# Loading one block of wo into lanes 0 to 63 by eleven small transfers

## The chip, the cores and the metric

The kernel runs on one core of one Trainium2 chip. The metric is the device time of one execution in microseconds (us). A core has five engines with an instruction queue each: TensorE (PE, with its weight loads as PEld), VectorE (DVE), ScalarE (ACT), GpSimd (POOL) and SyncE (SP). Data come from the chip's memory (HBM) into the on-chip SBUF, which has 128 lanes (partitions), by 16 DMA engines that work beside the five. SP and ACT start these transfers; each transfer is cut into packets, one for each contiguous piece.

## What is computed

One step of decoding for four sequences: attention over a cache of 4,096 keys and values with 32 heads of 128, beside a gated MLP, both added to the input.

```
xn  = layernorm(x)                                  # x: 4 x 640
q   = (xn @ wq) as 32 heads of 128
s   = q . k_cache * 128**-0.5                       # 4 x 32 x 4096
o   = softmax(s) . v_cache                          # 4 x 32 x 128
att = o.reshape(4, 4096) @ wo                       # wo: 4096 x 640
z   = gelu(xn @ w_in); z1, z2 = halves of z; z2 = layernorm(z2)
mlp = (z1 * (w_sp * z2 + b_sp)) @ w_out
out = x + att + mlp                                 # all inputs bfloat16
```

The two caches are 128 MiB each; all else together is some 14 MB. Every byte of them is read once.

## The kernel before

The heads are taken in eight groups of four (HG = 8, HT = 4). A tile is one group of one sequence: 32 tiles (NT) of K and 32 of V, each 128 lanes of 32,768 bytes (4,096 KB). They go through five buffers (KV_SLOTS) that K and V share. `load` issues one tile on SP's queue; `pump` issues the next ones of a fixed list as long as the buffer that each needs has been released (`used`).

The main loop runs over the 32 tiles i and is written out by hand for PE, DVE, ACT and SP. In each step DVE multiplies the K tile by the query and folds it in two halves (L400, L409), PE sums over the head dimension by matmuls with the identity (L418), DVE reduces (L429 to L442), ACT takes the exponentials (L453), and PE multiplies with an earlier V tile (`weighted`, L470). At the end of a step `pump` issues what has become possible.

Behind every fourth tile one group is finished. `group_pick` (L502) gathers its rows, `group_turn` (L513, L521) divides by the sum and transposes 32 by 32 on DVE, which leaves o_t with the head dimension on lanes, and `group_proj` (L530) multiplies by the group's 512 rows of wo and adds to out_ps, where x, the MLP and all groups are summed. The rows of one block of wo are spread so that lane p holds rows 4p to 4p+3: one contiguous piece of 5,120 bytes in each of 128 lanes (L155). `load_wo(j)` issues block j in step 4j+2, after `pump`; it has a pool of two buffers (WO_BUFS). The last block comes in four transfers, one for each head (L153), because the last group goes another way: the last V tile is loaded in four pieces (V_CUTS), its matmuls (L625) wait for each, and L530 follows.

Transfers that SP and ACT start use eight completion semaphores in turn; a transfer on a semaphore that is still in use by the one eight before it waits for that one to land.

Of the kernel before, what the change touches and what calls it, by code (L numbers as in the profile page):

```python
# [9 lines left out]
FP32 = mybir.dt.float32  # L10
BF16 = mybir.dt.bfloat16
# [3 lines left out]

KV_SLOTS = 5
EXTRA_K = (24, 28)
WO_BUFS = 2


@with_exitstack
def kernel(
# [14 lines left out]
    nc = tc.nc  # L37
    P = nc.NUM_PARTITIONS
    Bsz, Sq, D = A_x.shape
    _, H, S, Dh = A_k_cache.shape  # L40
# [8 lines left out]
    HT = 4  # L49
# [11 lines left out]
    NOH = D // 2  # L61
    QD = 32
# [5 lines left out]
    const = ctx.enter_context(tc.tile_pool(name="const", bufs=1))  # L68
    kv = ctx.enter_context(tc.tile_pool(name="kv", bufs=KV_SLOTS))
    wop = ctx.enter_context(tc.tile_pool(name="wop", bufs=WO_BUFS))  # L70
    work = ctx.enter_context(tc.tile_pool(name="work", bufs=1))
    small = ctx.enter_context(tc.tile_pool(name="small", bufs=2))
# [6 lines left out]
    def slot(name):  # L79
        return kv.tile([P, SLOT], BF16, tag="kv", name=name)  # L80

    x_bf = const.tile([Bsz, D], BF16)
    nc.scalar.dma_start(out=x_bf[:], in_=A_x.flatten_outer_dims())

    wq_v = A_wq.rearrange("(p c) n -> p c n", c=DC)
# [1 line left out]
    for c0, c1 in ((0, HT), (HT, DC)):  # L87
        t = slot("wq")[:, 0 : (c1 - c0) * HD].rearrange("p (c n) -> p c n", n=HD)
# [13 lines left out]
        out=w_out_sb[:, 0:NFF, :], in_=B_w_out[0 : NFF * P].rearrange("(p k) n -> p k n", k=NFF)  # L102
# [40 lines left out]
            n_loaded[0] += 1  # L143

    wo_tiles = {}

    def load_wo(j):
        wo_tiles[j] = wop.tile([P, HT, D], BF16, name="wo")
        rows = A_wo[j * HT * P : (j + 1) * HT * P]
        if j == HG - 1:  # L150
            by_head = rows.rearrange("(h p) n -> p h n", p=P)
            for hh in range(HT):
                nc.sync.dma_start(out=wo_tiles[j][:, hh, :], in_=by_head[:, hh, :])  # L153
            return
        nc.sync.dma_start(out=wo_tiles[j][:], in_=rows.rearrange("(p j) n -> p j n", j=HT))  # L155
# [2 lines left out]

    ident = const.tile([P, P], BF16)
    make_identity(nc, ident[:])  # L160
    ones_row = const.tile([1, P], FP32)
    nc.vector.memset(ones_row[:], 1.0)
    eps_tile = const.tile([P, 1], FP32)
    nc.vector.memset(eps_tile[:], eps)
    ones_sq = const.tile([P, P], FP32)
# [14 lines left out]
    for i in range(NSTAT):  # L180
# [5 lines left out]
        out=rstd[:], in_=mv[:, 1:2], func=ACT.Sqrt, bias=eps_tile[:Bsz], scale=1.0  # L186
# [4 lines left out]
        out=xn_bf[:],  # L191
# [9 lines left out]
    for c in range(DC):  # L201
        nc.tensor.transpose(
            out=xnT_ps[:, c, :], in_=xn_v[:, c, :], identity=ident[:Bsz, :Bsz]
# [7 lines left out]
    for r in range(QB):  # L211
        q_ps = ps_pv.tile([P, GW], FP32, tag="pv", name="q_ps")
        for c in range(DC):
            t, i = wq_parts[c]
            for g in range(CB):
                hg = r * CB + g
                nc.tensor.matmul(  # L217
                    out=q_ps[g * QD : (g + 1) * QD, :],
                    lhsT=xnT[:, c, :],
                    rhs=t[:, i, hg * GW : (hg + 1) * GW],  # L220
                    start=(c == 0),
                    stop=(c == DC - 1),
# [9 lines left out]
        out=hot[:],  # L232
        in_=ident[:].rearrange("p (g t m) -> p t m g", g=P // QD, t=2),
# [3 lines left out]
    for a in range(2):  # L237
        for t in range(2):
            nc.vector.tensor_copy(
                out=pick[:, a, :, :, 2 * a + t],  # L240
                in_=hot[:, t, :].rearrange("p (c h) -> p c h", c=CB),
# [8 lines left out]
    for half in range(2):  # L250
        nc.tensor.matmul(
            out=out_sum(half),
            lhsT=ident[:Bsz, :Bsz],
            rhs=x_bf[:, half * NOH : (half + 1) * NOH],
            start=True,
            stop=False,
# [11 lines left out]
    def gmlp():  # L268
        zz, gw, gt, gz, sq = (gm[n] for n in ("zz", "gw", "gt", "gz", "sq"))
        zT = ps_pv.tile([P, 2, NFC, Bsz], FP32, tag="pv", name="zT")  # L270
        for t in range(2):
            f1 = t * Fh + NFF * P
            w_t = w_in_sb[:, :, t * Fh : f1].rearrange("p c (f k) -> p c k f", k=NFF)
            for k in range(NFC):
                for c in range(DC):
                    nc.tensor.matmul(
                        out=zT[: P if k < NFF else FT, t, k, :],
                        lhsT=w_t[:, c, k, :] if k < NFF else w_in_sb[:, c, f1 : f1 + FT],
                        rhs=xnT[:, c, 0:Bsz],
                        start=(c == 0),  # L280
                        stop=(c == DC - 1),
# [5 lines left out]
            out=gw[:], in0=gw[:], scalar1=0.044715, scalar2=1.0, op0=ALU.mult, op1=ALU.add  # L287
# [3 lines left out]
            out=gt[:], in_=gw[:], func=ACT.Tanh, scale=math.sqrt(2.0 / math.pi)  # L291
        )
        nc.vector.tensor_scalar(
            out=gt[:], in0=gt[:], scalar1=1.0, scalar2=0.5, op0=ALU.add, op1=ALU.mult
# [5 lines left out]
        for src, at in ((gz[:, 1, :, :], 0), (sq[:], Bsz)):  # L300
            for k in range(NFC):
                nc.tensor.matmul(
                    out=s_ps[:, at : at + Bsz],
                    lhsT=ones_sq[:, 0:1],
                    rhs=src[:, k, :],
                    start=(k == 0),
                    stop=(k == NFC - 1),
                )
        st, ac = gm["st"], gm["ac"]
# [33 lines left out]
        )  # L343
        ac_ps = ps_m.tile([P, 2 * Bsz], FP32, tag="m", name="ac_ps")
        nc.tensor.matmul(
            out=ac_ps[:], lhsT=ones_row[:], rhs=ac[:], start=True, stop=True
        )
        ac_sb = work.tile([P, 2 * Bsz], FP32, name="ac_sb")
        nc.scalar.copy(out=ac_sb[:], in_=ac_ps[:])
# [161 lines left out]
    def group_turn(hg):  # L511
        o_n = small.tile([P, HT, QD], BF16, name="o_n")
        nc.vector.tensor_scalar(  # L513
            out=o_n[:].rearrange("p j q -> p q j"),
            in0=taken.pop(hg)[:].rearrange("p (q j) -> p q j", j=HT),
            scalar1=gr.pop(hg)[:, 0:1],
            scalar2=None,
            op0=ALU.mult,
        )
        o_t = small.tile([P, HT, QD], BF16, name="o_t")  # L520
        nc.vector.transpose(  # L521
            out=o_t[:].rearrange("p j q -> p (j q)"), in_=o_n[:].rearrange("p j q -> p (j q)")
        )
        gr[hg] = o_t[:, :, 0:Bsz]

    def group_proj(hg):
        o_n = gr.pop(hg)
        for hh in range(HT):
            for half in range(2):
                nc.tensor.matmul(  # L530
                    out=out_sum(half),
                    lhsT=o_n[:, hh, :],
                    rhs=wo_tiles[hg][:, hh, half * NOH : (half + 1) * NOH],
                    start=False,
                    stop=(hg == HG - 1 and hh == HT - 1),
                )
# [25 lines left out]
    with tc.manual_schedule(engines={E.PE, E.DVE, E.Activation, E.SP}):  # L562
        stage_q(0)
        stage_q(1)
        gmlp()
        used.update(occupants[:3])
        pump()
        for i in range(NT):
            j = turns.get(i)
            last = turns.get(i - 1, -1)  # L570
            product(i, 0)
            at(i - 1, row_sums, 1)
            at(i - 1, head_max)
            group(last, group_pick)
            fold_half(i, 0)
            at(i - 1, exps)
            sums(i, 0)
            group(last, group_turn)
            if i + 2 < NT:
                stage_q(i + 2)  # L580
            product(i, 1)
            due = [] if j is None else [j]
            if i == NT - 1:
                due += range(j + 1, NT - 2)
            for jj in due:
                consume(jj)
            row_sums(i, 0)
            fold_half(i, 1)
            sums(i, 1)
            group(last, group_proj)  # L590
            used.add(("k", i))
            pump()
            if i % Bsz == 2 and i // Bsz < HG - 1:
                load_wo(i // Bsz)
        load_wo(HG - 1)
        row_sums(NT - 1, 1)
        head_max(NT - 1)
        exps(NT - 1)
        hg, b = HG - 1, Bsz - 1
        o_ps = ps_m.tile([P, HT, Bsz], FP32, tag="m", name="o_last")  # L600

        def pick_last(a):
            o = taken.pop((hg, a))
            for c in range(CB):
                nc.tensor.matmul(
                    out=o_ps[:],
                    lhsT=o[:, c, :],
                    rhs=pick[:, a, c, :, 0:Bsz],
                    start=(a == 0 and c == 0),
                    stop=False,  # L610
                )

        pick_last(0)
        weighted(NT - 2, closing=True)
        take(hg, 1)
        den = ps_m.tile([P, HT, Bsz], FP32, tag="m", name="den_all")
        nc.tensor.matmul(
            out=den[:], lhsT=ones_sq[:], rhs=acc[hg % NACC][:, :, 0:Bsz], start=True, stop=True
        )
        rden = small.tile([P, HT, Bsz], FP32, name="rden_all")  # L620
        nc.vector.reciprocal(out=rden[:], in_=den[:])
        pick_last(1)
        pm = p_m[b][:].rearrange("p g (t c h) -> p g t c h", t=2, c=CB)
        for c in range(NC):
            nc.tensor.matmul(  # L625
                out=o_ps[:, :, b],
                lhsT=v_tiles[NT - 1][:, c, :],
                rhs=pm[:, c // CB, b % 2, c % CB, :],
                start=False,
                stop=(c == NC - 1),  # L630
            )
        o_n = small.tile([P, HT, Bsz], BF16, name="o_n_last")
        nc.vector.tensor_tensor(out=o_n[:], in0=o_ps[:], in1=rden[:], op=ALU.mult)
        gr[hg] = o_n
        group_proj(hg)

        res = work.tile([P, NOH], BF16, name="res")
        out_v = out.flatten_outer_dims()
        r0, r1 = slice(0, Bsz), slice(OG, OG + Bsz)
        nc.scalar.copy(out=res[r0], in_=out_ps[r0])  # L640
        nc.vector.tensor_copy(out=res[r1], in_=out_ps[r1])
        nc.scalar.dma_start(out=out_v[:, 0:NOH], in_=res[r0])
        nc.sync.dma_start(out=out_v[:, NOH:D], in_=res[r1])
# [30 lines left out]
```

## Time and profile before

| What | Value |
|---|---|
| Median of 3 runs (lowest, highest) | 666.81 us (666.65, 666.91) |
| The profiled execution, its own time | 666.78 us |
| Span of the profile, first to last instruction | 665.0 us |
| Busy: DVE, PE, ACT, POOL | 499.5, 309.9, 127.1, 4.7 us |
| HBM read over the span | 282.24 MB, 424 GB/s |
| K tiles: 32 transfers of 4,096 KB, issue to landing | 41.2 us (median) |
| V tiles: 31 transfers of 4,096 KB, issue to landing | 35.7 us (median) |
| wo blocks 0 to 6: 640 KB each, issue to landing | 42.3 us (median) |
| DVE at L400 idle for K to land | 104.3 us in 27 waits |

The span is what the profiler saw of the program's own instructions; some 1.8 us of the execution lie around it. Busy times are those of the instructions alone, so an engine can be idle in between and still be the one that the rest waits for. DMA shares are means over the 16 DMA engines: 1.00 means that all were at work, 0.5 that half of them were (or all half of the time), and a value a little above 1 comes from the overlap of neighbouring packets. q1 is the DMA queue that SP fills, q10 that of ACT; q8 and q14 carry the instruction streams of the engines. "Issue to landing" includes the time in which a transfer waits behind earlier ones.

### The profile page before, as it was taken

The page shows a single profiled execution, that of the slowest core. Times are in us where ns is not written, and L with a number is a line of the kernel's source. Part 1 is how long each engine was busy: PE and PEld are TensorE (multiplying, and loading weights), DVE is VectorE, ACT ScalarE, POOL GpSimd, SP SyncE. Part 2 cuts the span into 40 slices and gives each one's busy share as a digit, 9 for nine tenths or more (in the row PEclk, how much of TensorE's full clock was granted, in tenths as well). Part 3 has the DMA queues.
Part 4 walks back from the last instruction along what each step waited for, and adds up shares of the span by engine and source line. Part 5 has one row for each costly group of instructions (what it writes and reads, how often), then busy time and mean ns, then how long its engine had stood idle before and what let it go on. Part 6 is the DMA issues. An engine that isn't in the chain of part 4 may idle for free.

```text
span 665.0 us, 5142 instructions
## 1 busy us (share of the span) xinstructions
PE 309.9 (47%) x2033; PEld 130.3 (20%) x2033; DVE 499.5 (75%) x350; ACT 127.1 (19%) x441; POOL 4.7 (1%) x15
## 2 busy tenths in 40 slices
PE   2536443445436235553238443355443655338466
PEld 1312111211112111321113111131111312113124
DVE  2299797877788777788777697777787899776970
ACT  0302222102222111222111222111222122111121
POOL 2000000000000000000000000000000000000000
PEclk9656766877767777776776856788765678776575
DMA  9999999999999999999999999999999999999996
GB/s 367 430 440 417 434 436 426 433 430 429 436 420 440 426 430 437 426 431 428 432 433 424 435 434 424 438 421 440 427 430 436 423 436 426 433 432 430 431 430 274
DMA packets 11972, 282.58 MB, mean 425 GB/s; under 512 B 1344, under 2 KB 1964, under 8 KB 3244
## 3 DMA queue, kind: packets, MB, share of 16 engines
q1 hardware_dynamic: 11928, 282.25, 99.2%
q8 instruction: 16, 0.26, 0.2%
q14 instruction: 8, 0.07, 0.0%
q10 hardware_dynamic: 20, 0.01, 0.0%
HBM read 282.24 MB, written 0.01 MB: 424 GB/s over the span
## 4 chain that ended last, share of the span: by engine, by line
DMA 68%; DVE 23%; PE 6%; issue 2%; SPq 0%; DVEq 0%
DMA k_nat<-in_A_k_cache_dram 62%; DVE k_nat L400 12%; DVE k_nat L409 7%; PE s_ps L418 4%; DMA v_nat<-in_A_v_cache_dram 4%; DVE s_sb L429 2%; DMA wq<-in_A_wq_dram 2%; PE pv L470 1%; PE q_ps L217 1%; DVE m L438 0%; DVE mt L440 0%; DVE o_n L513 0%; DVE nm L442 0%; PE out_ps L530 0%; SPq L120 0%
## 5 line engine op out<-in xcount | busy, mean ns | idle before, releaser
L400 DVE TENSOR_TENSOR k_nat<-k_nat,qbc 128x8192 bf16<-128x8192 bf16 x64 | 282.7, 4417 | 104.6 <-DMA k_nat<-in_A_k_cache_dram 104.3
L418 PE MATMUL s_ps<-k_nat,ident 128*128 128x512 bf16 x512 | 183.8, 523 | 327.0 <-DVE k_nat L409 327.0
L418 PEld LDWEIGHTS <-ident 128*128 128x128 bf16 x512 | 62.3, 122 | 430.7 <-issue 356.8
L409 DVE TENSOR_TENSOR k_nat<-k_nat 128x4096 bf16<-128x4096 bf16 x64 | 146.0, 2281 | 0.0
L448 ACT ACTIVATE nb<-nm 128x1 f32<-128x1 f32 x32 | 6.5, 203 | 355.1 <-DVE nm L442 355.1
L470 PE MATMUL pv<-v_nat,pm 128*32 128x512 bf16 x992 | 71.0, 438 | 3.7 <-DMA v_nat<-in_A_v_cache_dram 3.7
L453 ACT ACTIVATE pm<-s_sb,nb 32x128 bf16<-32x128 f32 x128 | 71.7, 560 | 2.7
L394 ACT CAST qbc<-qbc_ps 32x128 bf16<-32x128 f32 x128 | 32.8, 256 | 133.1 <-PE qbc_ps L384 132.0
L429 DVE TENSOR_REDUCE s_sb<-s_ps 128x64 f32<-128x512 f32 x64 | 43.6, 682 | 3.1 <-PE s_ps L418 3.1
L470 PEld LDWEIGHTS <-pm 128*32 128x32 bf16 x992 | 25.9, 109 | 55.3 <-issue 36.9
L453 ACT ACTIVATION_READ_ACCUMULATOR pm<-s_sb,nb 32x1 f32 x128 | 30.1, 235 | 0.0
L502 PEld LDWEIGHTS o_ps<-o_rows,pick 128*128 128x128 f32 x112 | 20.1, 269 | 2.1 <-issue 1.4
L502 PE MATMUL o_ps<-o_rows,pick 128*128 128x128 f32 x112 | 19.5, 347 | 0.0
L384 PE MATMUL qbc_ps<-q_rows,ident 128*128 128x512 bf16 x32 | 17.5, 552 | 0.0
L482 ACT COPY o_rows<-pv 128x512 f32<-128x512 f32 x16 | 9.4, 585 | 27.5 <-PE pv L470 27.5
L494 DVE RECIPROCAL rden<-den 128x1 f32<-128x1 f32 x7 | 1.2, 168 | 15.6 <-PE den L486 15.6
L438 DVE TENSOR_REDUCE m<-s_sb 128x1 f32<-128x128 f32 x32 | 9.2, 286 | 1.1
L225 DVE CAST q_rows<-q_ps 128x512 bf16<-128x512 f32 x2 | 1.4, 692 | 10.6 <-PE q_ps L217 10.6
L440 DVE STREAM_TRANSPOSE mt<-m 128x32 f32<-128x32 f32 x32 | 6.8, 212 | 1.1
L217 PE MATMUL q_ps<-wq,xnT 128*32 128x512 bf16 x40 | 4.1, 552 | 7.3 <-DMA wq<-in_A_wq_dram 7.3
L442 DVE TENSOR_REDUCE nm<-mt 128x1 f32<-128x32 f32 x32 | 6.0, 186 | 1.1
L384 PEld LDWEIGHTS <-ident 128*128 128x128 bf16 x32 | 4.4, 141 | 8.6 <-issue 8.6
(83 smaller groups left out, 73.4 us busy)
## 6 DMA issues: line engine op xcount, KB each, us to landing
k_nat<-in_A_k_cache_dram SPq DMA_DIRECT2D x32, 4096.0 KB, 41.2
v_nat<-in_A_v_cache_dram SPq DMA_DIRECT2D x31, 4096.0 KB, 35.7
wo<-in_A_wo_dram SPq DMA_DIRECT2D x7, 640.0 KB, 42.3
wq<-in_A_wq_dram SPq DMA_DIRECT2D x1, 4096.0 KB, 12.8
w_sb<-in_B_w_in_dram SPq DMA_DIRECT2D x1, 2160.0 KB, 19.5
v_nat<-in_A_v_cache_dram SPq DMA_DIRECT2D x1, 2048.0 KB
wq<-in_A_wq_dram SPq DMA_DIRECT2D x1, 1024.0 KB, 14.8
v_nat<-in_A_v_cache_dram SPq DMA_DIRECT2D x1, 1024.0 KB
```

Of the source, the lines that this page charges most:

```text
L217: nc.tensor.matmul(out=q_ps[g * QD : (g + 1) * QD, :], lhsT=xnT[:, c, :], rhs=t[:, i, hg * GW : (hg + 1) * GW], start=(c == 0), stop=(c == ...
L384: nc.tensor.matmul(out=qb_ps[:], lhsT=ident[:, row : row + 1].to_broadcast([P, P]), rhs=q_rows[r][:], start=True, stop=True,)
L394: nc.scalar.copy(out=qbcs[i][ps, :], in_=qb_ps[ps, hh, :])
L400: nc.vector.tensor_tensor(out=half_of(i, half), in0=half_of(i, half), in1=qbcs[i][:, None, :].to_broadcast([P, HC, Dh]), op=ALU.mult,)
L409: nc.vector.tensor_tensor(out=t[:, :, 0:HD2], in0=t[:, :, 0:HD2], in1=t[:, :, HD2:Dh], op=ALU.add)
L418: nc.tensor.matmul(out=s[:], lhsT=ident[:], rhs=t[:, :, g * RW : (g + 1) * RW], start=(g == 0), stop=(g == n - 1),)
L429: nc.vector.tensor_reduce(out=scores[i][:, half * HC : (half + 1) * HC], in_=sums_ps.pop((i, half))[:], axis=AX.X, op=ALU.add,)
L438: nc.vector.tensor_reduce(out=m1[:], in_=scores[i][:], axis=AX.X, op=ALU.max)
L453: nc.scalar.activation(out=pm[ps, :, b % 2, :, hh], in_=s_sb[ps, :].rearrange("p (g c) -> p g c", c=CB), func=ACT.Exp, bias=nb[ps], scale= ...
L470: nc.tensor.matmul(out=pvs[hg, a][cg * QD : (cg + 1) * QD, :], lhsT=pm[:, g, :], rhs=v_nat[:, g * CB : (g + 1) * CB, :], start=(t == 0 and ...
L482: nc.scalar.copy(out=o[:].rearrange("p c d -> p (c d)"), in_=pvs.pop((hg, a))[:])
L502: nc.tensor.matmul(out=o_ps[:], lhsT=pick[:, a, c, :, :].rearrange("p h q -> p (h q)"), rhs=o[:, c, :], start=(a == 0 and c == 0), stop=(a ...
```

## The change

Block 1 of wo (`TALL`) no longer goes through the pool of wo buffers. It has a tile of its own, `wo_tall`, in lanes 0 to 63 (HP = 64), with two pieces (t) of four rows in each lane: lane l holds rows 4l to 4l+3 of the block and rows 256+4l to 256+4l+3. The block's 640 KB are the same. They are brought by eleven transfers on SP's queue. Eight sets of eight lanes are formed, a set being lanes four apart within one group of 32; five sets are loaded by one transfer each, and three are cut in two, into 7 and 1, 6 and 2, 5 and 3 lanes. `TALL_DUE` says how many are issued at the end of steps 1 to 6: 2, 1, 2, 2, 2, 2. `load_wo(1)`, in step 6, then does nothing.

`group_turn` copies, for that group, the upper 64 lanes of o_t down to lanes 0 to 63 by ACT (`o_up`), and `group_proj` runs over eight products of 64 lanes in place of four of 128, sixteen matmuls in place of eight. Beside it, three small things: x lives in the first four lanes of a 128-lane tile whose left half later takes the result (`res`), and a row of ones with its memset is dropped, since `ones_sq` holds the same values.

```diff
+TALL_DUE = {1: 2, 2: 1, 3: 2, 4: 2, 5: 2, 6: 2}
...
-    x_bf = const.tile([Bsz, D], BF16)
+    x_rows = const.tile([P, D], BF16)
+    x_bf = x_rows[0:Bsz, :]
...
+    TALL, HP, STEP = 1, P // 2, 4
+    wo_tall = const.tile([HP, 2, HT, D], BF16)
+    tall_v = A_wo[TALL * HT * P : (TALL + 1) * HT * P].rearrange(
+        "(t l j) n -> l t j n", t=2, j=HT
+    )
+    tall_lanes = []
+    for n, cut in enumerate((8, 8, 8, 8, 8, 7, 6, 5)):
+        first = n // STEP * QD + n % STEP
+        lanes = [first + STEP * m for m in range(QD // STEP)]
+        tall_lanes += [part for part in (lanes[:cut], lanes[cut:]) if part]
+
+    def load_tall():
+        lanes = tall_lanes.pop(0)
+        at = slice(lanes[0], lanes[-1] + 1, STEP)
+        nc.sync.dma_start(out=wo_tall[at], in_=tall_v[at])
 
     def load_wo(j):
+        if j == TALL:
+            return
...
-    ones_row = const.tile([1, P], FP32)
-    nc.vector.memset(ones_row[:], 1.0)
...
-            out=ac_ps[:], lhsT=ones_row[:], rhs=ac[:], start=True, stop=True
+            out=ac_ps[:], lhsT=ones_sq[0:1, :], rhs=ac[:], start=True, stop=True
...
         gr[hg] = o_t[:, :, 0:Bsz]
+        if hg == TALL:
+            o_up = small.tile([HP, HT, Bsz], BF16, name="o_up")
+            nc.scalar.copy(out=o_up[:], in_=o_t[HP:P, :, 0:Bsz])
+            gr["up"] = o_up
 
     def group_proj(hg):
         o_n = gr.pop(hg)
-        for hh in range(HT):
+        if hg == TALL:
+            terms = [
+                (o[0:HP, hh, :], wo_tall[:, t, hh, :])
+                for t, o in ((0, o_n), (1, gr.pop("up")))
+                for hh in range(HT)
+            ]
+        else:
+            terms = [(o_n[:, hh, :], wo_tiles[hg][:, hh, :]) for hh in range(HT)]
+        for hh, (o, w) in enumerate(terms):
...
                     stop=(hg == HG - 1 and hh == HT - 1),
...
                 load_wo(i // Bsz)
+            for _ in range(TALL_DUE.get(i, 0)):
+                load_tall()
...
-        res = work.tile([P, NOH], BF16, name="res")
+        res = x_rows[:, 0:NOH]
```

## The prediction

> **What bounds the kernel now.** The page's table of DMA queues and the chain of waits come first.
>
> ```profile
> q1 hardware_dynamic: 11928, 282.25, 99.2%
> q8 instruction: 16, 0.26, 0.2%
> q14 instruction: 8, 0.07, 0.0%
> ...
> DMA 68%; DVE 23%; PE 6%; issue 2%; SPq 0%; DVEq 0%
> ```
>
> SP's queue q1 keeps the 16 DMA engines busy for 99.2% of the span: the kernel streams 282 MB, and no compute engine is near that (DVE 75%). The reader should also see q8 and q14, where the instruction streams are fetched through the same 16 engines. Next, the stretches at the end, and the end of the chain:
>
> ```profile
> core 0: us, PE busy (x) PEld busy (x) DVE busy (x) ACT busy (x) POOL busy (x), PEclk, DMA share, GB/s
> ...
> 657.00:658.00 1.00, 1.00 (x44) 1.00 (x41) 0.00 (x0) 0.00 (x0) 0.00 (x0) 0.50 1.01 384
> 658.00:659.00 1.00, 1.00 (x38) 0.92 (x35) 0.00 (x0) 0.00 (x0) 0.00 (x0) 0.50 0.82 317
> 659.00:660.00 1.00, 0.47 (x16) 0.38 (x15) 0.00 (x0) 0.00 (x0) 0.00 (x0) 0.50 0.57 213
> 660.00:661.00 1.00, 0.59 (x16) 0.51 (x17) 0.17 (x1) 0.00 (x0) 0.00 (x0) 0.50 0.65 221
> 661.00:662.00 1.00, 1.00 (x8) 0.47 (x8) 0.00 (x0) 0.00 (x0) 0.00 (x0) 0.50 0.10 32
> ```
> ```profile
> 632.46 27.63 DMA v_nat<-in_A_v_cache_dram
> 660.09 0.05 issue
> 660.14 0.60 PE o_last L625 x16
> ...
> 661.00 1.36 PE out_ps L530 x8
> ```
>
> The DMA share (last column but one) falls from 1.01 to 0.57 at 659 and stays near 0.6 until 661: some six or seven of the 16 engines are done, and the kernel waits for the rest. Behind the last V piece (660.09) and the last wo piece (which L530's last matmuls need) come only about 5 us of matmul, copy and store. So the end is set by the DMA engine that finishes last.
>
> The trace holds start, length, bytes and queue of every DMA packet, but not its engine. Each engine works through the same list of sizes without a gap, so the packets can be strung into 16 chains, each packet behind the one that ended as it began. The moments by which the 16 chains end ahead of the last one, in us: 0, 0.03, 0.12, 0.14, 0.16, 0.18, 0.27 and 1.96 (these eight meet the q8 fetches, one every 40 us or so in a fixed round; 1.55 us lost at each; the last met one, the others two); 0.31 (three q14 fetches, 0.98 each) and 0.47 (four, 0.68 each); 2.59 (one q14 fetch); 3.48, 3.19, 3.08, 3.04, 2.45 (none). Nine engines are late, seven are early by 2 to 3.5. The mean is 1.34: no shift of bytes between engines can bring more than that.
>
> **The change part by part.** *The block.* It now comes in packets of the same 5,120 bytes, 128 as before, so the bytes and the packet prices stay; what moves is who carries them. Before, each engine carried 8. What a transfer of few lanes does is shown by the first loads: x_bf (4 lanes) left four data packets and four completions, each one-lane load one and one, 96 lanes 16 completions. So eight lanes take eight engines, two packets (the two halves, t) on each. The one-lane loads ran on a chain whose first wq packet began right at the end of an x_bf packet, so few-lane transfers start from one fixed engine, which I call the first; it is the chain at 3.08. The eleven transfers are five of 8 lanes, then 7+1, 6+2 and 5+3. Five eights give each of eight engines 10 packets. The 7, 6 and 5 add 2 to the first seven, six and five. The 2 and the 3 add 2 to the first two and three, and the single lane, split by its halves, 1 to the first two. That makes 21, 21, 18, 16, 16, 14, 12, 10 (sum 128), against 8 before: +13, +13, +10, +8, +8, +6, +4, +2, and −8 on the other eight.
>
> A 5,120-byte packet takes 196 to 202 ns in the records; eight with their completion 1.576 us, so 0.196 each, and 0.006 for each further completion. The shares are then +2.61, +2.61, +2.01, +1.61, +1.61, +1.21, +0.82, +0.42 us, and −1.58 for the rest. Bounds: a small transfer has no overhead beyond the 6 ns (lower end), or its packets stretch as the smallest ones did under crowding, 1,280 bytes in 55 to 88 ns, a factor 1.6 (upper: +4.2 on the first two). I take the lower: the row has the same size.
>
> [...]
>
> *Where it counts.* The end moves by the worst engine's share less its lead. The first engine: 2.61 − 3.08 = −0.47. The remaining seven shares fall on seven of the other 15 engines, of which only six are early, so at least one late engine is among them; if the eight that meet q8 are all spared, the two q14 engines (0.31 and 0.47) both are. On the second place a late engine gives +2.1 to +2.6, on the third +1.5 to +2.0, on the fourth or fifth +1.1 to +1.6, on the last three from −0.05 to +1.2. A random draw over the 15 gives a mean of 2.1 with nine tenths between 1.4 and 2.6; if the eight q8 engines are the unloaded half, the mean is 1.5. I take +2.1: one late engine near the front.
>
> *SP.* Ten more issues of 0.33 to 0.43 us (the K/V and wo rows): about 4 us over six steps of 20 us. Nine of the eleven wait for the load issued eight before on their semaphore, some two steps back. A wait of that kind stands in the trace:
>
> ```profile
> SPq L153 <- DMA v_nat<-in_A_v_cache_dram: 15.9, 2, 9.4
> ...
> k_nat<-in_A_k_cache_dram SPq DMA_DIRECT2D x32, 4096.0 KB, 41.2
> wo<-in_A_wo_dram SPq DMA_DIRECT2D x7, 640.0 KB, 42.3
> ```
>
> Queued behind them on SP are the next V and K loads, which DVE and PE wait for. A K load lands 41.2 us after its issue and needs 9.7 (4,096 KB at the 431 GB/s of the stretch from 300 to 500 us), so about 31 us of work stand ahead of any new issue; SP may be some 9 us late and no DMA engine runs dry. Without that cover it would cost up to 9 us. POOL's queue is not touched. Should SP's longer stream need one more q14 fetch, its engine loses 0.7 of its lead of 2.59. The last tall pair goes out at the step in which L155 issued this block, and it is needed at L530:
>
> ```profile
> 160.87 0.43 SPq L155 DMA_DIRECT2D wo<-in_A_wo_dram  x1
> ...
> 219.75 0.71 PE L530 MATMUL out_ps<-wo,o_t 128*4 128x320 bf16 x8
> ```
>
> That is 59 us for some 42 of landing: nothing.
>
> *The rest.* Eight more matmuls at L530 (0.3 us each, 2.4 together if nothing hid them), one ACT copy (nearest row L394, 0.26), one memset less at the start (below 0.2, beside the 12.8 us that wq takes), and x and the result in another tile with the same transfers. PE (47%) and ACT (19%) idle under the stream at 220 us, where the DMA share is 1.00: nothing.
>
> Sum: 666.78 for the profiled execution (span 665.0 and 1.8 around it) + 2.1 = 668.9; the median of the runs is 666.81, 0.03 away.
>
> **The rivals.** *B, only light places are late.* The late engines among the eight sit in the last three places: −0.05 to +1.2, centre +0.5, 667.3. For: three of seven places are light. Against: the other four places must then all have drawn early ones.
>
> *C, not slower: the transfers use all 16 engines.* An 8-lane transfer has 16 packets; if these went one to each engine, the five eights would load all alike (5), and the six parts add 6 on the first and 0 on the last ones: +3 packets (0.6 us) on early places, −3 on the last. The end moves by 0 to +0.6, centre +0.2: 667.0. It decides if packets and not lanes are dealt out. Against: four lanes of x_bf, one packet each, cannot tell the two apart, but 128 lanes went 8 to an engine.
>
> *D, balance.* The late engines are all among the unloaded ones, because the new program's instruction streams are fetched through other engines. Then the rest fall by 1.58 and the first engine decides at −0.47: 666.3. Against: the round of q8 was fixed through two turns.
>
> *E, dearer small transfers or a dry queue*: from +2.6 to +4.2, 670.
>
> *G, the lanes' side counts.* If what a lane's group takes in is the limit and not the engine, then leftovers carried by the first engines still slow the owners of those lanes, and every one of the eight pays +8: a late one ends at 1.61 − 0.31 = +1.3 at least, 668.1 to 668.4. For it nothing in the trace: an engine that was 1.3 us behind wrote four 1,280-byte packets in 55 ns each while the other 15 ran K, no longer than before it. [...]
>
> **How the numbers follow.** Likeliest, +1.1 to +2.6 (G inside it): 0.75. B 0.10, C 0.07, D 0.05, E 0.03. About 0.2% (1.33 us) is what a measurement of this kernel can tell from no change. Of the 0.75 some 0.06 lie below that, so slower is 0.69 + 0.03 = 0.72; B, C, 0.06 and 0.03 of D are the same, 0.26; faster 0.02, since a full balance gives 1.34 at most. The range starts inside C at 667.1 and ends at 669.6 (+2.8), leaving out D, E and half of C.
>
> **What would show it.** In the changed profile the bytes stay 282 MB; eleven rows of wo_tall appear with 10 to 80 KB; the DMA share at the end falls earlier and lower (more engines done), and a tail of one or two busy engines (share 0.06 to 0.15) of about 2 us precedes the end. In chains, eight engines are 1.58 earlier and two 2.6 later. Wrong: a DMA share that stays high to the end (D), equal chains (C), a share below 0.9 between 90 and 200 us (E).

## The result and the profile after

The changed kernel takes 669.46 us (median of 4 runs, 669.36 to 669.66) where the kernel before takes 666.81: 2.65 us more, a ratio of 1.0040 with a 95% interval of 1.0026 to 1.0054. Its profiled execution took 669.66 us with a span of 667.8.

The page first: the table of DMA queues (packets, MB, share of 16 engines) and the chain that ended last.

```profile
q1 hardware_dynamic: 11977, 282.25, 98.8%
q8 instruction: 16, 0.26, 0.2%
q14 instruction: 8, 0.07, 0.0%
...
DMA 74%; DVE 19%; PE 4%; issue 2%; SPq 0%; DVEq 0%
```

The bytes of q1 are the same 282.25 MB and the instruction fetches are the same 16 and 8. The share of q1 fell from 99.2% to 98.8%: the same work, with more empty engine time in a longer span. It is at the end that this time lies. The windows of the changed kernel's last microseconds (busy time of each engine with its count; then PE's clock, DMA share, GB/s):

```profile
core 0: us, PE busy (x) PEld busy (x) DVE busy (x) ACT busy (x) POOL busy (x), PEclk, DMA share, GB/s
657.00:658.00 1.00, 1.00 (x18) 0.98 (x18) 0.00 (x0) 0.00 (x0) 0.00 (x0) 1.00 0.88 341
...
659.00:660.00 1.00, 0.54 (x21) 0.45 (x17) 0.00 (x0) 0.00 (x0) 0.00 (x0) 0.50 0.76 280
660.00:661.00 1.00, 0.78 (x29) 0.78 (x30) 0.00 (x0) 0.00 (x0) 0.00 (x0) 0.50 0.39 147
661.00:662.00 1.00, 0.78 (x26) 0.66 (x22) 0.00 (x0) 0.00 (x0) 0.00 (x0) 0.50 0.27 99
662.00:663.00 1.00, 0.30 (x11) 0.26 (x10) 0.00 (x0) 0.00 (x0) 0.00 (x0) 0.50 0.29 90
663.00:664.00 1.00, 0.73 (x17) 0.48 (x15) 0.17 (x1) 0.00 (x0) 0.00 (x0) 0.50 0.06 22
```

Before, the share stood near 0.6 until 661 and was 0.10 from there on: nine engines ended together. Now it falls to 0.39 at 660, is 0.27 (four engines) at 661 and 0.29 at 662, and ends at 0.06, one engine of 16. To read such a view, one has to know that a window counts each packet whole, in the window where it begins. That is what lifts a share above 1, and not the overlap of neighbouring packets, which is 3 to 4 ns. The 0.29 holds 0.08 of a late instruction fetch of 1.3 us; without it about three engines are at work there. The chain of waits of the changed kernel says who waited for it (start, duration, what):

```profile
634.41 28.29 DMA v_nat<-in_A_v_cache_dram
662.70 0.05 issue
662.75 0.60 PE o_last L656 x16
...
663.60 1.37 PE out_ps L559 x5
```

The last V piece ends at 662.70 where it ended at 660.09 (+2.61), and what follows, 5.1 us to the end of the span, took 4.9 before. Counted from the records of single packets, each by its own start and end and without instruction fetches, the number of DMA engines at work in each half microsecond, back from the end of the last data packet, is:

```
us before the end     4.0-3.5  3.5-3.0  3.0-2.5  2.5-2.0  2.0-1.5  1.5-1.0  1.0-0.5  0.5-0
before                  16.7     15.1     12.2     10.4      9.6      9.7      9.7     6.2
changed                  7.1      5.4      4.9      4.2      4.3      2.8      1.1     1.1
```

For its last microsecond the changed kernel waits for one engine. Strung into 16 chains as in the prediction, the records say which. "Place" is the rank among the eight engines that carry the block; "lead" is how far a chain ends ahead of the last one:

```
place  packets  instruction fetches on this engine      lead, us
  1      21     none                                      2.70
  2      21     four q14 (0.68 us each before)            0
  3      18     none                                      3.64
 4, 5    16     three q14 on one, one q14 on the other    1.2 and 3.4
 6, 7   14, 12  q8, two each                              1.14 and 1.35
  8      10     none                                      4.25
 others   0     q8 on six, none on two                    3.97 to 7.0
```

The eleven transfers make the shares of the forecast, packet for packet. The engine at the second place is the one with four q14 fetches. Before, it was 0.47 ahead of the last one; now it is the last.

### The profile page after: what moved, and what is told of

It reads as the page before. It is cut to its first block, busy times and chain, and to the rows that moved or that the text cites. A ratio compares the mean times of both kernels' runs of the same rounds, so it can differ in the third digit from the quotient of the medians.

```text
span 667.8 us, 5169 instructions
## 1 busy us (share of the span) xinstructions
PE 305.1 (46%) x2041; PEld 128.3 (19%) x2041; DVE 498.8 (75%) x349; ACT 127.5 (19%) x442; POOL 4.7 (1%) x15
## 3 DMA queue, kind: packets, MB, share of 16 engines
q1 hardware_dynamic: 11977, 282.25, 98.8%
## 4 chain that ended last, share of the span: by engine, by line
DMA 74%; DVE 19%; PE 4%; issue 2%; SPq 0%; DVEq 0%
DMA k_nat<-in_A_k_cache_dram 68%; DVE k_nat L417 10%; DVE k_nat L426 6%; DMA v_nat<-in_A_v_cache_dram 4%; PE s_ps L435 3%; DMA wq<-in_A_wq_dram 2%; DVE s_sb L446 2%; PE q_ps L234 1%; DVE m L455 0%; DVE o_n L530 0%; DVE mt L457 0%; PE pv L487 0%; DVE nm L459 0%; PE out_ps L559 0%; SPq L122 0%
## 5 line engine op out<-in xcount | busy, mean ns | idle before, releaser
L435 PEld LDWEIGHTS <-ident 128*128 128x128 bf16 x512 | 62.1, 121 | 434.8 <-issue 360.1
L487 PE MATMUL pv<-v_nat,pm 128*32 128x512 bf16 x992 | 69.3, 429 | 5.2 <-DMA v_nat<-in_A_v_cache_dram 5.1
```

Source lines behind the costliest of these rows:

```text
L435: nc.tensor.matmul(out=s[:], lhsT=ident[:], rhs=t[:, :, g * RW : (g + 1) * RW], start=(g == 0), stop=(g == n - 1),)
L487: nc.tensor.matmul(out=pvs[hg, a][cg * QD : (cg + 1) * QD, :], lhsT=pm[:, g, :], rhs=v_nat[:, g * CB : (g + 1) * CB, :], start=(t == 0 and ...
```

## The experiments

All kernels were timed in five rounds beside the kernel before. It took 666.88 us (24 runs) beside the small loads and the compute alone, 666.95 (7 runs) beside the last two kernels and 666.82 (15 runs) beside the others. Diffs are against the changed kernel.

### Equal shares: eight transfers of eight lanes

```diff
-TALL_DUE = {1: 2, 2: 1, 3: 2, 4: 2, 5: 2, 6: 2}
+TALL_DUE = {1: 2, 2: 1, 3: 1, 4: 1, 5: 1, 6: 2}
...
-    for n, cut in enumerate((8, 8, 8, 8, 8, 7, 6, 5)):
+    for n, cut in enumerate((8, 8, 8, 8, 8, 8, 8, 8)):
```

> Eight transfers of eight lanes, none cut: each of the first eight DMA engines carries 16 packets of the block, the others none. Theory (the end is set by the engine that finishes last, share less lead): +1.61 on each of the eight, and the latest of them that the changed kernel's chains show there has a lead of 0.18, so +1.4 us, 668.2. Rival (each small transfer costs something by itself, wherever it runs): 8/11 of the +2.65 of the changed kernel, +1.9, 668.7. Rival (the leftovers are all of it): 666.8 to 667.2.

Measured: 668.21 us (667.97 to 668.72, 11 runs), ratio 1.0020 (1.0012 to 1.0029). Eight chains carry 16 packets. The four that end last, within 0.63 us, are the three-fetch q14 engine, two q8 engines and the four-fetch q14 engine; no engine without the block is nearer than 2.85. In the trace of this kernel, the windows near the end show the four:

```profile
660.00:661.00 1.00, 0.59 (x16) 0.51 (x16) 0.00 (x0) 0.00 (x0) 0.00 (x0) 0.50 0.27 102
661.00:662.00 1.00, 0.59 (x16) 0.51 (x16) 0.00 (x0) 0.00 (x0) 0.00 (x0) 0.50 0.32 107
662.00:663.00 1.00, 0.73 (x7) 0.37 (x7) 0.17 (x1) 0.00 (x0) 0.00 (x0) 0.50 0.11 37
```

A share of 0.27 to 0.32 is four to five engines (0.06 of the 0.32 is a late instruction fetch), until the last microsecond begins. The cost, 1.39, is 8 packets more (1.57) less the lead that the worst engines among the first eight had before (0.03 to 0.31). So about half of the loss of 2.65 is the halving of the carriers, and the rest (1.26) comes with the cuts into 7+1, 6+2 and 5+3.

### Twice the load on the same eight engines

```diff
+TALL_DUE = {1: 2, 2: 1, 3: 1, 4: 1, 5: 1, 6: 2, 12: 2, 13: 3, 14: 3}
+TALLS = (1, 3)
...
+    for b in TALLS:
+        for n in range(8):
+            first = n // STEP * QD + n % STEP
+            tall_lanes.append((b, [first + STEP * m for m in range(QD // STEP)]))
```

> As even_eights, with block 3 brought in the same way, in steps 12 to 14. Theory: a second +1.61 on each of the first eight engines, so +3.0 us in all, 669.8. Rival (a stall in the first 200 us, or the second half's relief, decides): no more than even_eights, 668.2.

Measured: 669.99 us (669.91 to 670.13, 5 runs), ratio 1.0046 (1.0032 to 1.0059): the second block added 1.78 where 8 packets make 1.57. The carriers (the engines that bring the block) that were late in the run above are late here too (leads 0, 0.43, 0.50, 0.71), and the engines without a block are 6.1 to 9.1 ahead. The cost goes with the packets on the worst engine. The load is long over by then (the last of these transfers is issued at 343.4 us, in step 14 of 32), and its 1.78 us still stand at the end.

### Twelve small loads on the first engine alone, and on the first two

Block 1 is loaded as before here. Twelve transfers of 5,114-byte pieces, read from wo into a tile that nothing uses, come on top: of one lane each (LANES = 1), or of two lanes four apart (LANES = 2).

```diff
+    LANES, CUT = 1, 2557
+    spots = [(l, t) for l in (0, 1, 2, 3, QD, QD + 1) for t in range(2)]
...
+        l, t = spots.pop(0)
+        at = slice(l, l + STEP * (LANES - 1) + 1, STEP)
+        flat = wo_tall[at, t].rearrange("p j n -> p (j n)")
+        nc.sync.dma_start(
+            out=flat[:, 0:CUT], in_=A_wo.rearrange("(p j) n -> p (j n)", j=HT)[at, 0:CUT]
+        )
```

> Block 1 loaded and used as in the kernel before; added are twelve one-lane transfers of 5,114 bytes into a spare tile, into lanes of the first engine, two a step in steps 1 to 6. Theory: all twelve run on the first engine, 12 x 0.2 = 2.5 us, under its lead of 3.08: no change, 666.8. Rival (each small transfer costs by itself, 2.65/11): +2.9, 669.7. Rival (bytes alone): 0.2.

> As first_alone, but each of the twelve transfers takes two lanes, four apart, and so the first two engines with a lane each. Theory: the second engine gets 2.5 us and has a lead of 0.47 (it is the one with the four fetches of ACT's stream): +2.0 us, 668.8. Rival (small transfers cost by themselves): as first_alone. Rival (the second engine is an early one): 666.8.

Measured: one lane 667.12 us (666.92 to 667.39, 11 runs), ratio 1.0002 (0.9993 to 1.0011); two lanes 668.76 us (668.5 to 668.88, 8 runs), ratio 1.0027 (1.0017 to 1.0037). Twelve pieces more on the first engine cost nothing that can be told; its lead fell from 3.08 to 0.93. The same twelve issues with a second lane cost 1.88 us: 12 × 0.196 less the second engine's lead of 0.47 is 1.88. The windows at the end, one lane:

```profile
660.00:661.00 1.00, 0.53 (x16) 0.50 (x16) 0.00 (x0) 0.00 (x0) 0.00 (x0) 0.50 0.72 239
661.00:662.00 1.00, 0.73 (x9) 0.44 (x7) 0.17 (x1) 0.00 (x0) 0.00 (x0) 0.50 0.18 61
```
Two lanes:

```profile
661.00:662.00 1.00, 0.31 (x12) 0.22 (x9) 0.00 (x0) 0.00 (x0) 0.00 (x0) 0.50 0.22 72
662.00:663.00 1.00, 0.73 (x20) 0.55 (x18) 0.17 (x1) 0.00 (x0) 0.00 (x0) 0.50 0.07 23
```

With one lane the end is nearly that of the kernel before: about ten engines and a late instruction fetch (0.72), then 0.18, where the kernel before has 0.65, also with a fetch, and 0.10. With two lanes a single engine (0.07) works a microsecond longer; its chain is the one with the four q14 fetches (that these bring ACT's stream, as was expected, is not in the trace). This pair tells the mechanism from every other one that counts issues, bytes or completions, since the two kernels differ by one lane of a transfer.

### The compute of the change without its transfers

The block is loaded as before. The ACT copy stays, and eight matmuls of 64 lanes on a tile of zeros are added to the eight of 128.

```diff
-TALL_DUE = {1: 2, 2: 1, 3: 2, 4: 2, 5: 2, 6: 2}
+TALL_DUE = {}
...
+    wo_zero = const.tile([HP, HT, D], BF16)
+    nc.gpsimd.memset(wo_zero[:], 0.0)
...
+                    (o_n[:, hh, :], wo_tiles[hg][:, hh, :]),
+                    (up[:, hh, :], wo_zero[:, hh, :]),
```

> The compute part alone, and more than all of it: block 1 loaded as in the kernel before, its eight matmuls kept, and the ACT copy of the upper lanes and eight matmuls of 64 lanes on a tile of zeros added. Theory (all hidden under the stream): 666.8, within 0.2. Rival (PE or ACT carry part of the change): +0.5 or more.

Measured: 666.96 us (666.63 to 667.61, 11 runs), ratio 1.0001 (0.9992 to 1.0010). The copy, the eight more matmuls and the moved tile of x and the result cost nothing that can be told.

### One transfer of 64 lanes

```diff
-TALL_DUE = {1: 2, 2: 1, 3: 2, 4: 2, 5: 2, 6: 2}
+TALL_DUE = {6: 1}
...
-        lanes = tall_lanes.pop(0)
-        at = slice(lanes[0], lanes[-1] + 1, STEP)
-        nc.sync.dma_start(out=wo_tall[at], in_=tall_v[at])
+        nc.sync.dma_start(out=wo_tall[:], in_=tall_v)
```

> [...] Theory A (only the carrying engine pays): no change, 666.8. [...] Rival (only the lanes count): +1.58 - 0.18, +1.4, 668.2.

Measured: 670.85 us (670.7 to 671.25, 5 runs), ratio 1.0060 (1.0047 to 1.0073). Every theory was too low. All 16 chains carry 8 packets of the block, as before the change, and their order at the end is the old one (leads 0 to 3.9); so no engine is loaded more than another, and yet 4 us are gone. The windows of this kernel while the block comes in:

```profile
196.00:200.00 4.00, 1.00 (x18) 0.42 (x7) 2.96 (x3) 0.59 (x1) 0.00 (x0) 1.00 0.98 374
200.00:204.00 4.00, 3.67 (x24) 2.62 (x23) 0.00 (x0) 0.00 (x0) 0.00 (x0) 1.00 1.08 210
204.00:208.00 4.00, 0.00 (x0) 0.10 (x1) 3.33 (x1) 0.00 (x0) 0.00 (x0) 1.00 0.95 297
```

The DMA share is at its full value, 1.08 and 0.95, but the bytes fall to 210 and 297 GB/s, against 431 in the steady stretch. (With each packet's bytes spread over its own time, the engines are busy all of both windows and move 198 and 275 GB/s.) An engine that counts as busy here moves fewer bytes, because its packets take longer: the block's 128 packets took 407 ns in the mean instead of 198, and packets of K next to them up to 3,301 ns instead of 1,216. Spread over 16 engines, the block's packets lost 1.7 us (128 × 209 ns / 16) and the K and V packets beside them 2.1 us (33.8 / 16, from the table in the next part), together 3.8 of the 4.0 measured.

### The same shares, written to other lanes

Three kernels keep the equal shares (16 packets on each of the first eight engines) and change only which lanes a transfer fills: lanes 64 to 127, four apart (o_t's lower half is then copied up, and the matmuls run on lanes 64 to 127); lanes 0 to 63, two apart; lanes 0 to 63, next to each other. The diffs leave out the two lines of the equal shares, which are as above, and for the upper lanes those of the copy and the matmuls.

```diff
-    wo_tall = const.tile([HP, 2, HT, D], BF16)
+    wo_rows = const.tile([P, 2, HT, D], BF16)
+    wo_tall = wo_rows[HP:P]
```
```diff
-    TALL, HP, STEP = 1, P // 2, 4
+    TALL, HP, STEP = 1, P // 2, 2
...
-        first = n // STEP * QD + n % STEP
-        lanes = [first + STEP * m for m in range(QD // STEP)]
+        first = n // STEP * 16 + n % STEP
+        lanes = [first + STEP * m for m in range(8)]
```
```diff
-        lanes = [first + STEP * m for m in range(QD // STEP)]
+        lanes = [8 * n + m for m in range(8)]
...
-        at = slice(lanes[0], lanes[-1] + 1, STEP)
+        at = slice(lanes[0], lanes[-1] + 1)
```

The upper lanes came first:

> As even_eights, but the block lies in lanes 64 to 127; still eight transfers of eight lanes. Theory A (only the carrier pays, and eight-lane transfers always run on the first eight engines): as even_eights, 668.2. [...]

Measured: 674.9 us (673.89 to 675.81, 4 runs), ratio 1.0119 (1.0105 to 1.0133), a wide miss again. The 16 packets are on the same eight engines as in the even-eights kernel; only the lanes differ, and K packets take 1,400 to 2,240 ns on the carriers and on the other eight. The rows of wo that each transfer reads, and their order, are also those of the even eights, so where the data come from is not the reason. That suggested a theory for the two misses together, which the last two runs were to test. A stretch in it is the set of lanes that one engine fills in the even eights, if a transfer's lanes are dealt out in order: four neighbouring lanes and the four that lie 32 above, eight stretches in lanes 0 to 63. That a stretch has a rate of its own was the author's estimate and is not shown.

> [...] Theory (a stretch of lanes takes in about what one engine delivers, 210 GB/s over 8 of them in the 64-lane transfer, so engines that share one slow each other): clearly slower than the 668.2 us of the even eights; three writers at a time on a stretch give up to 3 x 0.196 us a packet, 16 of them less the 1.57 us spared: up to +7.9, so 670 to 675 us. Rival (which engine carries a packet decides alone, and lanes 64 to 127 are costly for a reason of their own): 668.2 within 0.7 us.

> [...] Theory (engines that write into one stretch of lanes share its rate): more than with lanes two apart, since five writers share a stretch at a time; 672 to 679 us, DMA share at 1.0 while GB/s drop in the stretch from 90 to 200 us. Rival (the carrying engine decides alone): 668.2 within 0.7 us, and the same as with lanes two apart. [...]

Measured: two apart 674.0 us (673.41 to 675.52, 4 runs), ratio 1.0102 (1.0086 to 1.0119); next to each other 676.09 us (675.82 to 676.22, 4 runs), ratio 1.0136 (1.0121 to 1.0151). Both times lie in the range that the theory gave, in its order, and the rival's 668.2 is out. (Who pays is another matter; see below.) The same window of four kernels while the first two transfers come in (DMA share and GB/s are the last two columns). Four apart:

```profile
100.00:104.00 4.00, 0.53 (x3) 0.13 (x2) 1.10 (x1) 0.00 (x0) 0.00 (x0) 1.00 1.02 434
```
Two apart:

```profile
100.00:104.00 4.00, 0.54 (x3) 0.14 (x2) 0.11 (x1) 0.00 (x0) 0.00 (x0) 1.00 0.98 303
```
Next to each other:

```profile
100.00:104.00 4.00, 0.50 (x3) 0.01 (x1) 0.00 (x0) 0.00 (x0) 0.00 (x0) 1.00 1.08 238
```
Upper lanes, four apart:

```profile
100.00:104.00 4.00, 0.92 (x5) 0.20 (x2) 0.00 (x0) 0.00 (x0) 0.00 (x0) 1.00 0.98 270
```

DMA is "busy" in all four, and moves 434, 303, 238 and 270 GB/s (with bytes spread over each packet's time 430, 318, 242 and 299, at a share of 1.01 in all four). The packets show where the time goes. For the packets of the block and for the K and V packets between 80 and 230 us, summed over all engines:

```
kernel                 displaced packets   the block's first 32     K and V packets, sum of
                       (estimate)          packets, mean (max) ns   time less 1,216 ns each, us
before                        -                                             5.5
even eights                   0              197 (202)                      6.0
changed kernel               12              197 (202)                     13.2
lanes two apart             112              316 (599)                     67.5
lanes next to each other    112              444 (835)                     93.2
upper lanes                   -              319 (408)                     87.5
one transfer of 64      64 or more           331 (492)                     39.3
```

The trace does not hold the lane of a packet, so the second column is an estimate, worked out from the packet counts. By these (21, 21, 18 down to 10 in the changed kernel) a transfer of a few lanes loads the first engines, as many as it has lanes; if its lanes are also dealt to them in order, which no trace shows, each engine's lanes in the even eights are known. Displaced is a packet of the block that another engine brings into such a lane. Of the kernel before and of lanes 64 to 127 the estimate says nothing. With lanes two apart, two engines of a transfer then write into one stretch, with neighbouring lanes four. The even eights lose next to nothing against the kernel before (6.0 and 5.5 us), the kernels with 64 displaced packets and more and the upper lanes lose most. The count alone does not set the size: for the same 112 packets the K and V packets lose 62.0 us with lanes two apart and 87.7 with neighbouring ones. For each displaced packet they lose 0.53 to 0.78 us of engine time (33.8 / 64 at most, 62.0 / 112, 87.7 / 112, and 7.7 / 12 in the changed kernel, the 5.5 of the kernel before taken off); in the upper lanes it is 0.64 for each packet of the block (82.0 / 128).

One thing does not fit the theory. If engines that write into one stretch slowed only each other, those that write elsewhere would have gone on at 1,216 ns: of K's 128 lanes a transfer of the block fills only eight. None did. In the packet records all 16 engines have a K or V packet of over 1,450 ns in flight at one moment (125.4 us with lanes two apart, 104.1 with neighbouring lanes); in the even eights it is never more than one. Strung into chains, the eight without the block lost 3.9 to 4.5 us each with lanes two apart, the carriers 3.9 to 5.1. So the whole stream is held up beside displaced packets, also on engines that carry none of the block. That the lanes decide is shown, by equal shares at 434, 303, 238 and 270 GB/s; why the engines without the block wait is not, nor that a stretch has a rate or an engine of its own, and that the two times fell into the theory's range is in part luck.

## Why the prediction was right

The forecast was 668.9 us inside 667.1 to 669.6; measured 669.46. Point by point:

- *The end is set by the DMA engine that finishes last, and a shift of bytes between engines moves it by share less lead.* Shown three times: one lane against two lanes (+0.24 and +1.88), equal shares (+1.39), and the changed kernel's own chains.
- *Who carries how much.* 21, 21, 18, 16, 16, 14, 12, 10, as predicted. That the first engine can take its 21 (lead 3.08) held: it still ends 2.70 ahead.
- *"One late engine near the front", +2.1.* It was the second place, where the four q14 fetches are: 2.61 − 0.47 = +2.14. Measured were +2.63 at the last data packet, counted from the first instruction, and +2.65 in the medians. The place was luck: the prediction could not tell which engine stands where, and its +2.1 was the mean of a random draw (and one late engine near the front), which happens to equal 2.61 − 0.47. By its size the result lies 0.05 above the band held likeliest, at the foot of E's, and 0.14 us inside the range.
- *The mis-sized term.* The share was priced at 0.196 us a packet, with nothing for the company. With twelve pieces and no leftovers the same engine cost what the sum says (1.88). In the changed kernel it also carries leftovers, pieces cut off the sets of lanes, which by the estimate above lie in lanes that the sixth to eighth place fill in the even eights. Beside these its own K packets took 1,506 and 1,441 ns instead of 1,216, which is 0.5 us and covers the rest of the 2.65. That this is the whole rest is a sum; no run has the changed kernel's shares without its leftovers.
- *G, the lanes' side counts.* Held to be without any evidence, but the lanes count, beside the carriers' shares rather than in their place. The eighth place ran K packets of 1,414, 1,671 and 1,611 ns while leftovers came in, which by the same estimate went to lanes that it fills in the even eights. It is not a matter of that place alone: engines that carry none of the block lost about 0.3 us each too (0.53 against 0.23 above 1,216 ns each between 80 and 230 us). No run shows that a lane's group is the limit or has an owner, and so none shows G's +8 for every one of the eight; the runs show equal shares at 668.21 to 676.09 us by the choice of lanes alone. The row used against G (a late engine's four 1,280-byte packets, 55 ns each among K) came from a transfer of 96 lanes and says nothing of one of few lanes. The 12 displaced packets went with 7.7 us of engine time in all (13.2 less 5.5), most of it on engines with a lead to spare.
- *If the q8 eight are all spared.* They were not: six of them are among the unloaded eight, two at the sixth and seventh place. They were light places, 1.14 and 1.35 ahead, and decided nothing.
- *SP.* An issue of a tall transfer took not 0.33 to 0.43 us but 0.64 to 0.89, as the tile's own instructions show (durations min/median/max in ns, first and last start in us):

```profile
L162 SPq DMA_DIRECT2D wo_tall<-in_A_wo_dram x11: 640/715/886, 65.9 to 165.2; - x11
L559 PE MATMUL out_ps<-wo_tall,o_t x8: 294/296/296, 222.4 to 222.8; 64*4 64x320 bf16 x8
```

  Beside it the matmuls of 64 lanes, from 222.4 on, long after the last issue at 165.2. The cover was as wide as forecast: the DMA share stayed at 0.98 to 1.03 from 90 to 200 us, and SP's own waits were short at the new line:

```profile
SPq L122 <- DMA k_nat<-in_A_k_cache_dram: 26.5, 5, 7.4
...
SPq L162 <- DMA k_nat<-in_A_k_cache_dram: 1.4, 1, 1.4
```

  The tall loads themselves waited 1.4 us once; five loads behind them at L122 waited for a K tile (26.5 us in all), while the waits for a V tile there fell from 290.9 to 274.2, without a gap in the stream.
- *Compute at nothing.* Held (666.96 against 666.88).
- *The tail.* Forecast were one or two busy engines for about 2 us; it was four or five until 1.5 us before the end, about three for half a microsecond and one for the last. Only the second place had been named; the q14 engine with 16 packets and the two q8 engines with 14 and 12 end 1.1 to 1.4 us before it.
- *B, C, D and E.* The late engine that decides was not at a light place (B). Chains with 21 and with 0 packets exclude transfers over all 16 engines (C) and a balance (D). The small transfers of the even eights cost no more than their packets, 197 ns each, and the stream did not run dry (E): its DMA share was 0.98 to 1.03 from 90 to 200 us.

No arrangement tried is faster than the kernel before, and the mean lead of 1.34 us, 0.2%, bounds what any shift of bytes between the engines could give, an estimate from the chains before. Not tried: fewer instructions, so that the late engines fetch less, and transfers with unequal shares and no displaced packets.

## What to carry to other kernels

In a kernel that streams at full rate, look at the DMA engines one by one, at least by the DMA share of the last microseconds: here a transfer of eight lanes loaded the same eight of the 16 engines each time, and what counted was how late the latest of these already was (+0.24 us for twelve pieces on an engine 3.08 ahead, +1.88 with one 0.47 ahead). A full DMA share is no proof of a full rate: between 100 and 104 us a share of 0.98 to 1.08 went with 238 to 434 GB/s, so read the GB/s beside it. If a transfer must have fewer than 128 lanes, try more than one choice of lanes: with eight lanes four apart the stream went on at 434 GB/s, two apart at 303, and with eight neighbouring ones it fell to 238.

## What the runs showed of the hardware

- Instruction fetches made the DMA engines unequal. Strung into chains, the fetches in q8 (16 KB each) went round eight engines, 1.55 us lost at each; those in q14 (8 KB) stayed on three others, four, three and one of them, 0.68 to 0.98 us each. Whose instructions a fetch brings is not in the trace. Over the run that is up to 3.5 us between engines that were given equal bytes.
- A transfer of eight lanes ran on the same first eight engines whether it filled lanes 0 to 63 or 64 to 127. One of fewer lanes ran on as many of them, from the first on (21, 21, 18 down to 10 packets in the changed kernel); which lane goes to which engine is not in the trace.
- Equal shares took 668.21 us with lanes four apart, 674.0 two apart, 676.09 next to each other and 674.9 in lanes 64 to 127, the K and V packets of all 16 engines slower in the last three. For each displaced packet they lost 0.53 to 0.78 us of engine time, summed over the engines, where a packet of the even eights takes 0.2 in all. Which packets are displaced is the estimate above; the times are from the traces.
- The issue of a small transfer on SP took 0.64 to 0.89 us in the changed kernel with lanes four apart, 0.68 to 0.87 for eight lanes two apart and 0.29 to 0.37 for eight neighbouring lanes.
